# Block-causal attention and two MLPs on one core: attention scores of the later queries as three f32r products, under a new planned order

## The chip, the cores and the metric

The kernel runs on one core of one Trainium2 chip. The metric is the device time of one execution in microseconds, as the median of repeated runs. A profile of one execution gives the rows that are read below.

## The reference

Attention over 4 batches, 8 heads, 576 positions and head width 64, with a mask that is causal by blocks of 64 positions. Its output goes through an MLP with softplus and then through a second MLP with a softmax-weighted activation (SoLU) and a layer norm. All of it is in f32.

```python
scores = scale * np.matmul(q, k.transpose(0, 1, 3, 2))          # [4, 8, 576, 576], scale = 1/8
mask = block_i >= block_j                                        # blocks of 64
scores = np.where(mask, scores, -1000000000.0)
attn = np.exp(scores - np.max(scores, axis=-1, keepdims=True))
attn = attn / (np.sum(attn, axis=-1, keepdims=True) + 1e-09)
x = np.matmul(attn, v)                                           # then (2304 tokens, 512)
h = x @ w_in                                                     # 512 -> 2048
g = np.maximum(h, 0.0) + np.log1p(np.exp(-np.abs(h)))
y = g @ w_out                                                    # 2048 -> 512
h = y @ w_in2                                                    # 512 -> 1024
e = np.exp(h - max(h)); sm = e / (sum(e) + 1e-09); solu = h * sm
ln = (solu - mean(solu)) / np.sqrt(var(solu) + 1e-06) * g_ln
out = ln @ w_out2                                                # 1024 -> 512
```

## The kernel before

The work is cut into tasks, each a few instructions of one engine. A planner (`Plan.run`) takes every task with a duration, its dependencies and a rank, plays the engines forward in time, and always gives a free engine the ready task of lowest rank. The result is one fixed order for each engine's queue. A rank is a number of the task's group (`RANK`: a start and a step per unit), plus an offset of the function (`OFF`), plus a local number. So the tables `RANK` and `OFF` at the head of the file set the order of everything, and each queue then runs in order.

The MLP matmuls are f32r products of split numbers: a value is held as a high part rounded to f32r and a low part that is the rest, and a product is high x high, high x low and low x high, accumulated in PSUM. The weights are split on the chip in `Piece`: one load on SyncE's queue, an Abs on ScalarE, three bit operations on VectorE, a rounding copy and a subtraction.

The stages, in order of time:

- Units A (16, one for each batch and pair of heads): attention of the queries 0 to 255. At the same time the 32 pieces of the first MLP's weights are split, and the first pairs of the MLP run.
- Units C (16): attention of the queries 256 to 575. Each handles two heads that sit in partitions 0 to 63 and 64 to 127 of one tile, `qkC`, of 960 columns: 256 columns of q for the blocks 0 and 1 of 128 queries, 128 columns for the last 64 queries of both heads, laid out block-diagonally, and 576 columns of k. Block 0 (i = 0) sees 384 keys, block 1 sees 512, block 2 (i = 2, the block 8 of 64 queries of both heads) sees 576.
- Pairs (72): two rows of 128 of the first MLP's hidden width for a chunk of 256 tokens: `a` is w1 x (tile `hp`), then softplus on ScalarE and VectorE, then `b` (tile `acc`). They are in the queues between the steps of the attention from early on, since their ranks stand behind those of the units.
- Pieces U1 and U2 split the second MLP's weights, once the units C have freed their memory (`open_u`). Then come 18 steps `Tok` of 128 tokens each: `h`, the SoLU and norm, a transpose, and `op`.

Inside a unit C the path is: load `qkC` (two buffers), scores (`mm_qk`) into the one score tile `S` of two PSUM banks, mask, row maximum (`max`, line 406), exponent with its sum (`exp`, line 416), reciprocal, scaling (`norm`), transpose on TensorE through the one tile `T` (`tr`), copy to `ps`, product with v into `O` (`pv`), and the split of the result into the MLP's input `xt`. In blocks 0 and 1 the two heads write one bank each, from 64 rows each. All of it is plain f32 on TensorE. Line 203 is the helper `mm` that records nearly every matmul, line 209 and line 211 are the helper `copy` on ScalarE and VectorE.

Of the kernel before, what the change touches and what calls it, by code (L numbers as in the profile page):

```python
# [11 lines left out]
F32R = mybir.dt.float32r  # L12
I32 = mybir.dt.int32
AF = mybir.ActivationFunctionType
ALU = mybir.AluOpType
AX = mybir.AxisListType
# [2 lines left out]


OFF = {
    "Pair.a": -64.28, "Pair.b": 5.61, "Pair.do_gh": -507.04, "Piece.bits0": 97.37, "Piece.do_lo@P": -245.38,
    "Piece.do_lo_g": 483.40, "Tok.a": 249.83, "Tok.x_hi": -287.82, "UnitA.x_hi": 218.85, "Tok.tr": -74.68,
    "Tok.bm": 218.59, "UnitC.pv": 72.58, "UnitC.tr": -127.84, "Pair.stt": -176.06, "Pair.do_gl": -341.89,
}
RANK = {
# [3 lines left out]
    "Tok": (3472.49, -21.973),  # L30
}
MARGIN = {
    "PE": 600.0, "ACT": 100.0, "DVE": 100.0, "POOL": 100.0,
# [2 lines left out]
B, H, S, D = 4, 8, 576, 64  # L36
# [9 lines left out]
WC = (384, 512, 576)  # L46
# [5 lines left out]
class Plan:  # L52
# [8 lines left out]
    def add(self, eng, dur, rank, fn, deps=(), lat=None):  # L61
        t = _Task()
        t.key = key_of(fn)

        t.alts = dict(eng) if isinstance(eng, dict) else {eng: dur}
        name, i = t.group = self.group
        t.local = rank
        t.rank = rank + RANK[name][0] + RANK[name][1] * i + OFF.get(t.key, 0.0) + OFF.get(t.key + "@" + name, 0.0)
        t.eng, t.fn, t.n, t.done = None if len(t.alts) > 1 else eng, fn, len(self.tasks), False
        t.lat = (self.LAT + (120.0 if eng == "PE" else 0.0)) if lat is None else lat  # L70
        t.users, t.left, t.ready = [], 0, 0.0
        for d in deps:
            if d is not None:
                d.users.append(t)
                t.left += 1
        self.tasks.append(t)
        return t
# [5 lines left out]
    def chain(self, eng, rank, steps, deps):  # L83
        for dur, fn in steps:
            t = self.add(dur if isinstance(dur, dict) else eng, dur, rank, fn, deps)
            deps = [t]
        return t
# [83 lines left out]
def key_of(fn):  # L171
    while isinstance(fn, partial):
        fn = fn.func
    return ".".join(fn.__qualname__.split(".")[-2:])


def act_ns(n):
    return 70.0 + 0.833 * n


def dve_ns(n, per=1.04):
    return 70.0 + per * n
# [6 lines left out]
def dma_ns(nbytes, n=1):  # L189
    return max(50.0 + nbytes / 360.0, 550.0 * n)  # L190
# [3 lines left out]
def body(ctx: ExitStack, tc: tile.TileContext, qk, qkA, vP, vA, w1, w2, u1, u2, gln, out):  # L194
    nc = tc.nc
    PE, ACT, DVE, POOL, SP = nc.tensor, nc.scalar, nc.vector, nc.gpsimd, nc.sync
    plan = Plan()
    XTB, LAG = 3, 2
    add, chain = plan.add, plan.chain
    DMA_LAT = 1700.0  # L200

    def mm(out, lhsT, rhs, start, stop):
        PE.matmul(out, lhsT, rhs, start=start, stop=stop, skip_group_check=True)  # L203
# [3 lines left out]
    def copy(e, out, a):  # L207
        if e == "ACT":
            ACT.activation(out, a, AF.Copy)  # L209
        else:  # L210
            ENG[e].tensor_copy(out, a)  # L211

    def at_of(lst, i):
        return lst[i] if 0 <= i < len(lst) else None
# [15 lines left out]
    state = {}  # L230
# [88 lines left out]
    def xfree(c):  # L319

        return [t for u in pairs if u.c == c - XTB for t in (u.t_a0, u.t_a1)]
# [3 lines left out]
    class UnitC:  # L325
# [6 lines left out]
        def plan(self, prev, opened):  # L332
            p1, p2 = at_of(prev, len(prev) - 1), at_of(prev, len(prev) - 2)

            def g(u, *names):
                return [getattr(u, x) for x in names] if u else []

            self.t_qk = add("SP", dma_ns(128 * 3840), -12, self.load_qk, [opened] + g(p1, "t_qk") + g(p2, "t_mm"), DMA_LAT)
            self.t_v = add("SP", dma_ns(327680), -8, self.load_v, [opened, self.t_qk] + g(p2, "t_pv") + g(p1, "t_v"), DMA_LAT)
            sfree, tfree = (p1.sfree, p1.tfree) if p1 else ([], [])  # L340
            self.t_tr, cps = [[], [], []], []
            for i, w in enumerate(WC):
                r, heads = 7.0 * i, (0, 1) if i < 2 else (0,)
                self.t_mm = t = add("PE", (800, 1000, 1060)[i], r, partial(self.mm_qk, i), [self.t_qk] + sfree)
                if i < 2:
                    t = add("DVE", 140, r, partial(self.mask, i), [t])
                t = chain("DVE", r, ((dve_ns(w * len(heads)), partial(self.max, i)), (140, partial(self.scale, i))), [t])
                sfree = []
                for j in heads:
                    sfree.append(add("ACT", 250 + .833 * w, r, partial(self.exp, i, j), [t] + sfree + (p1.t_tr[i] if p1 else [])))  # L350
                t = chain("DVE", r, ((140, partial(self.den0, i)), (140, partial(self.den1, i))), sfree)
                for j in heads:
                    n = add("DVE", 70 + .55 * w, r, partial(self.norm, i, j), [t])
                    for part in ((0,) if i < 2 else (0, 1)):
                        m = 3 + i if i < 2 else (4, 1)[part]
                        x = add("PE", 60 + 110 * m, r + 5, partial(self.tr, i, j, part), [n] + tfree)
                        self.t_tr[i].append(x)
                        c = add({"ACT": 110 + 107 * m, "DVE": 90 + 133 * m}, None, r + 4, partial(self.copy, i, j, part), [x] + g(p1, "t_pv"))
                        tfree = [c]
                        cps.append(c)  # L360
            self.sfree, self.tfree = sfree, tfree
            self.t_pv = add("PE", 2272, 24, self.pv, cps + [self.t_v] + (p1.t_x if p1 else []))
            self.t_x, ta, tb, done = [], None, None, 0
            while done < NB:
                c, off = divmod(self.b * NB + done, CT)
                c += B
                w = min(NB - done, CT - off)
                args = (c, off, done, w)
                ta = add({"ACT": act_ns(w) + 40, "DVE": dve_ns(w)}, None, 22, partial(self.x_hi, *args), [self.t_pv, ta] + xfree(c))
                tb = add("DVE", dve_ns(w), 22, partial(self.x_lo, *args), [ta, tb])  # L370
                xparts.setdefault(c, []).append(tb)
                self.t_x.append(tb)
                done += w
            prev.append(self)

        def load_qk(self):

            self.qk = self.t([128, 960], "qkC")
            SP.dma_start(out=self.qk, in_=qk[self.b, self.pr])

        def load_v(self):
            self.v = self.t([128, 2, 5, D], "v")
            SP.dma_start(out=self.v, in_=vP[self.b, :, 2 * self.pr:2 * self.pr + 2])

        def scores(self, i):
            S, w = state["S"], WC[i]
            return S[:, :, 0:w] if i < 2 else S.rearrange("p a b -> p (a b)")[:, None, 0:w]

        def mm_qk(self, i):
            S, w, qk = state["S"], WC[i], self.qk  # L390
            if i < 2:
                for j in range(2):
                    h = slice(64 * j, 64 * j + 64)
                    mm(S[:, j, 0:w], qk[h, 128 * i:128 * i + 128], qk[h, 384:384 + w], True, True)
            else:
                mm(S[:, 0, :], qk[:, 256:384], qk[:, 384:896], True, True)
                mm(S[:, 1, 0:64], qk[:, 256:384], qk[:, 896:960], True, True)

        def mask(self, i):

# [2 lines left out]
        def max(self, i):  # L403
            self.m, self.den = self.t([128, 2], "mC", 3), self.t([128, 2], "dC", 3)
            n = 2 if i < 2 else 1
            DVE.tensor_reduce(out=self.m[:, 0:n], in_=self.scores(i), axis=AX.X, op=ALU.max, negate=True)  # L406
            self.n = n

        def scale(self, i):
# [3 lines left out]

        def exp(self, i, j):
            m, den, _ = self.stat[i]
            ACT.activation(state["eC"][i][:, j, :], self.scores(i)[:, j, :], AF.Exp, scale=0.125,  # L416
                           bias=m[:, j:j + 1], accum_out=den[:, j:j + 1])

        def den0(self, i):
            _, den, n = self.stat[i]  # L420
# [327 lines left out]
    for kind, f in todo:  # L748
        src, t, done = (w1[f], w1t[f], w1ready) if kind == "w1" else (w2[f * 128:f * 128 + 128, :], w2t[f], w2ready)
        p = Piece(src, w_of(t, 0), w_of(t, 1))  # L750
# [23 lines left out]
    for f in range(8):  # L774
        p = Piece(u1[f], u1_of(0, f), u1_of(1, f))
# [4 lines left out]
    for f in range(8):  # L780
        p = Piece(u2[f * 128:f * 128 + 128, :], w_of(w1t[6 + f], 0), w_of(w1t[6 + f], 1), gcol[:, f:f + 1])
        n = len(upieces) % 3
# [226 lines left out]
```

## Time and profile before

| | |
|---|---|
| Time, median of 3 runs | 818.53 us (815.85 to 818.89) |
| The profiled execution's own time | 818.25 us |
| Span of its instructions | 816.5 us |
| Time around the span | 1.75 us |
| Mean granted TensorE clock, as a share of 2.4 GHz | 0.991 |

The rows of the trace speak of the span. An f32 matmul stands in the rows as two matmul instructions and two weight loads (PEld), an f32r matmul as one of each; both types are labelled f32 there, so the tile names tell them apart: `S`, `T`, `O` and the tiles `R` and `r` of the units A hold f32 products, `hp`, `acc`, `h` and `op` f32r ones. A matmul's duration in a row is longer than the distance to the next one, since matmuls overlap; the distance of the starts is what a matmul costs.

### The profile page before, as it was taken

Reading aid. Unit: us, or ns where it says so; the run is one execution under the profiler, and the core shown is the slowest. Engines: PE = TensorE matmul, PEld = TensorE weight load, DVE = VectorE, ACT = ScalarE, POOL = GpSimd, SP = SyncE. Lnnn points to the kernel's source line nnn. Section 1 sums busy time; section 2 is a strip of 40 time slices with the busy share of each in tenths; the row PEclk is TensorE's granted clock in tenths of the full one; section 3 lists DMA queues with packets and bytes.
Section 4 is the critical chain, followed back from the end, with each engine's and each line's share of the span. In section 5 each row is a group of like instructions: output and inputs, shape, how many; then the busy total and the mean of one; then the engine's idle time right before and its main releaser. Section 6 shows DMA issues by size and latency. Waiting matters only on the chain.

```text
span 816.5 us, 14229 instructions
## 1 busy us (share of the span) xinstructions
PE 790.5 (97%) x5656; PEld 684.6 (84%) x5656; DVE 546.0 (67%) x1273; ACT 391.9 (48%) x863; POOL 0.7 (0%) x6
## 2 busy tenths in 40 slices
PE   5689999999999999999999999999999999999998
PEld 3478889998888788888887889999988888888887
DVE  6989999575666665665565652776949576766661
ACT  5566775554555545455554543645623232322232
POOL 0000000000000000000000000000000000000000
PEclk9799999999999999999999999999999999999999
DMA  5636551202121112112211100326301111110001
GB/s 166 214 119 192 175 165 63 92 10 79 49 83 41 42 42 67 41 42 71 61 41 41 58 3 26 105 78 207 117 27 39 51 39 53 39 51 27 26 26 51
DMA packets 31201, 59.63 MB, mean 73 GB/s; under 512 B 2848, under 2 KB 14368, under 8 KB 31136
## 3 DMA queue, kind: packets, MB, share of 16 engines
q1 hardware_dynamic: 31136, 58.74, 22.5%
q8 instruction: 44, 0.72, 0.4%
q14 instruction: 21, 0.17, 0.1%
HBM read 49.29 MB, written 9.44 MB: 72 GB/s over the span
## 4 chain that ended last, share of the span: by engine, by line
PE 80%; DVE 13%; DMA 3%; ACT 2%; issue 2%; SPq 0%; ACTq 0%; DVEq 0%
PE hp L203 19%; PE acc L203 18%; PE op L203 12%; PE h L203 11%; PE S L203 6%; PE O L203 5%; PE T L437 4%; PE tp L905 2%; PE R L203 2%; DVE a L283 2%; DMA raw<-in_w_dram 2%; DVE a L279 1%; DVE t L641 1%; DVE gl L649 1%; PE r L203 1%
## 5 line engine op out<-in xcount | busy, mean ns | idle before, releaser
L203 PE MATMUL hp<-xt,w 128*128 128x256 f32 x1728 | 218.9, 281 | 1.1 <-DVE t L641 1.0
L203 PEld LDWEIGHTS hp<-xt,w 128*128 128x128 f32 x1728 | 205.9, 189 | 5.4 <-issue 3.4
L203 PE MATMUL acc<-gh,w 128*128 128x256 f32 x768 | 150.3, 286 | 0.0
L203 PEld LDWEIGHTS acc<-gh,w 128*128 128x128 f32 x768 | 122.4, 189 | 13.0 <-issue 12.5
L203 PE MATMUL acc<-gl,w 128*128 128x256 f32 x384 | 107.0, 279 | 0.6 <-DVE gl L649 0.6
L203 PE MATMUL op<-w,w2w 128*128 128x512 f32 (+1 forms) x456 | 102.3, 381 | 0.0
L203 PE MATMUL h<-u,w 128*128 128x512 f32 x432 | 100.9, 390 | 0.0
L203 PEld LDWEIGHTS h<-u,w 128*128 128x128 f32 x432 | 80.7, 188 | 16.5
L203 PEld LDWEIGHTS op<-w,w2w 128*128 128x128 f32 x456 | 81.5, 188 | 15.3
L632 ACT ACTIVATE t<-hp 128x512 f32<-128x512 f32 x72 | 42.9, 596 | 79.3 <-PE hp L203 74.5
L209 ACT ACTIVATE ps<-T 128x512 f32<-128x512 f32 (+1 forms) x77 | 42.7, 554 | 75.0 <-PE T L437 60.3
L203 PEld LDWEIGHTS acc<-gl,w 128*128 128x128 f32 x384 | 72.7, 189 | 0.8 <-DVE gl L649 0.8
L641 DVE SCALAR_TENSOR_TENSOR t<-hp,t 128x512 f32<-128x512 f32 x72 | 49.4, 686 | 26.4 <-ACT t L638 26.0
L416 ACT ACTIVATE eC<-S,mC 128x384 f32<-128x384 f32 (+2 forms) x80 | 51.7, 653 | 11.6 <-DVE mC L410 11.5
L406 DVE TENSOR_REDUCE mC<-S 128x2 f32<-128x768 f32 (+2 forms) x48 | 46.9, 976 | 7.9 <-PE S L203 7.2
L203 PE MATMUL S<-qkC 64*128 64x384 f32 (+2 forms) x192 | 51.9, 533 | 0.0
L649 DVE TENSOR_TENSOR gl<-t,gh 128x512 fp32r<-128x512 f32 x72 | 49.6, 689 | 2.8 <-ACT gh L209 1.5
L203 PE MATMUL acc<-gh,w2w 128*128 128x256 f32 x256 | 50.2, 285 | 0.9 <-DVE gh L211 0.7
L857 ACT ACTIVATE e<-h,mx 128x1024 f32<-128x1024 f32 x18 | 20.1, 1116 | 55.1 <-PE tp L905 48.6
L203 PEld LDWEIGHTS acc<-gh,w2w 128*128 128x128 f32 x256 | 40.5, 188 | 6.9 <-issue 5.5
L638 ACT ACTIVATE t<-t 128x512 f32<-128x512 f32 x72 | 45.4, 630 | 2.0
L635 ACT ACTIVATE t<-t 128x512 f32<-128x512 f32 x72 | 45.4, 631 | 1.1
(149 smaller groups left out, 1050.4 us busy)
## 6 DMA issues: line engine op xcount, KB each, us to landing
raw<-in_w_dram SPq DMA_DIRECT2D x32, 512.0 KB, 3.9
qkC<-in_qk_dram SPq DMA_DIRECT2D x16, 480.0 KB, 3.4
raw_u<-in_u_dram SPq DMA_DIRECT2D x11, 512.0 KB, 3.5
v<-in_vP_dram SPq DMA_DIRECT2D x16, 320.0 KB, 3.0
x2s<-stg SPq DMA_DIRECT2D x18, 256.0 KB, 2.2
xr<-x2s SPq DMA_DIRECT2D x18, 256.0 KB, 3.1
qkA<-in_qkA_dram SPq DMA_DIRECT2D x16, 256.0 KB, 3.3
out_dram<-ob SPq DMA_DIRECT2D x15, 256.0 KB, 2.0
```

The source lines that it names most:

```text
L203: PE.matmul(out, lhsT, rhs, start=start, stop=stop, skip_group_check=True)
L209: ACT.activation(out, a, AF.Copy)
L283: DVE.scalar_tensor_tensor(out=self.a, in0=self.raw[:, :, 0], scalar=29, in1=self.a, op0=ALU.logical_shift_right, op1=ALU.bitwise_or)
L406: DVE.tensor_reduce(out=self.m[:, 0:n], in_=self.scores(i), axis=AX.X, op=ALU.max, negate=True)
L416: ACT.activation(state["eC"][i][:, j, :], self.scores(i)[:, j, :], AF.Exp, scale=0.125, bias=m[:, j:j + 1], accum_out=den[:, j:j + 1])
L437: PE.transpose(T[:, 128 * k:128 * k + 128], e[:, 128 * k:128 * k + 128], ident)
L632: ACT.activation(self.t, self.hp, AF.Abs)
L635: ACT.activation(self.t, self.t, AF.Exp, scale=-1.0)
L638: ACT.activation(self.t, self.t, AF.Ln, bias=1.0)
L641: DVE.scalar_tensor_tensor(out=self.t, in0=self.hp, scalar=0.0, in1=self.t, op0=ALU.max, op1=ALU.add)
L649: DVE.tensor_sub(self.gl, self.t, self.gh)
L857: ACT.activation(self.e, self.hh, AF.Exp, bias=self.mx, accum_out=self.ss)
```

## The change

In the units C, q and k are split after their load into a high part (`qk_hi`, a rounding copy of 960 columns on ScalarE or VectorE, as the planner finds) and a low part (`qk_lo`, a subtraction of 960 columns on VectorE). Raw tile, high part and low part have one buffer each, where the raw tile had two. The load of the next unit's tile waits for this unit's low part. The high part of the next unit waits for the last score matmul of this one.

Each score product becomes three f32r products, high x high, high x low, low x high, alternating between the two heads in blocks 0 and 1. Block 2's 576 keys are halved: 288 columns in each of the two banks, where 512 stood in one and 64 in the other. Maximum and exponent of block 2 read the two halves through one pattern. The planner's durations for the three score steps are new, and so are nearly all numbers of `RANK` and `OFF`.

The units A keep plain f32 scores. The diff:

```diff
@@ -19,15 +19,16 @@
 
 
 OFF = {
-    "Pair.a": -64.28, "Pair.b": 5.61, "Pair.do_gh": -507.04, "Piece.bits0": 97.37, "Piece.do_lo@P": -245.38,
-    "Piece.do_lo_g": 483.40, "Tok.a": 249.83, "Tok.x_hi": -287.82, "UnitA.x_hi": 218.85, "Tok.tr": -74.68,
-    "Tok.bm": 218.59, "UnitC.pv": 72.58, "UnitC.tr": -127.84, "Pair.stt": -176.06, "Pair.do_gl": -341.89,
+    "Pair.a": -160.87, "Pair.b": -32.19, "Pair.do_gh": -103.91, "Piece.bits0": 139.36, "Piece.do_lo@P": -201.40,
+    "Piece.do_lo_g": 267.76, "Tok.a": 141.06, "Tok.x_hi": -460.68, "UnitA.x_hi": 408.37, "Tok.tr": -394.45,
+    "Tok.bm": 359.77, "UnitC.pv": 348.22, "UnitC.tr": -288.31, "Pair.stt": -191.35, "Pair.do_gl": -445.21,
+    "UnitC.qk_lo": -290.12,
 }
 RANK = {
-    "first": (278.93, 20.397), "A0": (-641.43, 96.996), "A1": (-4066.20, 24.379), "A2": (-152.64, -0.844),
-    "A3": (-1221.38, -173.545), "P0": (3437.70, -107.962), "P": (247.97, -35.750), "C": (692.49, 11.636),
-    "Pair0": (7.78, -1.510), "Pair": (1879.52, 20.653), "U1": (2411.63, 26.547), "U2": (1151.70, -31.129),
-    "Tok": (3472.49, -21.973),
+    "first": (278.93, 20.397), "A0": (636.85, 83.080), "A1": (-4008.02, 57.487), "A2": (-200.66, 24.018),
+    "A3": (-1158.93, -177.493), "P0": (3522.23, -182.270), "P": (108.24, -25.537), "C": (1333.72, -23.955),
+    "Pair0": (-27.93, 4.604), "Pair": (1577.17, 27.249), "U1": (3142.36, 101.962), "U2": (864.20, 12.958),
+    "Tok": (4285.47, -27.327),
 }
 MARGIN = {
     "PE": 600.0, "ACT": 100.0, "DVE": 100.0, "POOL": 100.0,
@@ -335,13 +336,15 @@
             def g(u, *names):
                 return [getattr(u, x) for x in names] if u else []
 
-            self.t_qk = add("SP", dma_ns(128 * 3840), -12, self.load_qk, [opened] + g(p1, "t_qk") + g(p2, "t_mm"), DMA_LAT)
+            self.t_qk = add("SP", dma_ns(128 * 3840), -12, self.load_qk, [opened] + g(p1, "t_ql"), DMA_LAT)
+            self.t_qh = add({"ACT": act_ns(960), "DVE": dve_ns(960, .52)}, None, -6, self.qk_hi, [self.t_qk] + g(p1, "t_mm"))
+            self.t_ql = add("DVE", dve_ns(960), -6, self.qk_lo, [self.t_qh])
             self.t_v = add("SP", dma_ns(327680), -8, self.load_v, [opened, self.t_qk] + g(p2, "t_pv") + g(p1, "t_v"), DMA_LAT)
             sfree, tfree = (p1.sfree, p1.tfree) if p1 else ([], [])
             self.t_tr, cps = [[], [], []], []
             for i, w in enumerate(WC):
                 r, heads = 7.0 * i, (0, 1) if i < 2 else (0,)
-                self.t_mm = t = add("PE", (800, 1000, 1060)[i], r, partial(self.mm_qk, i), [self.t_qk] + sfree)
+                self.t_mm = t = add("PE", (600, 760, 860)[i], r, partial(self.mm_qk, i), [self.t_ql] + sfree)
                 if i < 2:
                     t = add("DVE", 140, r, partial(self.mask, i), [t])
                 t = chain("DVE", r, ((dve_ns(w * len(heads)), partial(self.max, i)), (140, partial(self.scale, i))), [t])
@@ -375,26 +378,34 @@
 
         def load_qk(self):
 
-            self.qk = self.t([128, 960], "qkC")
-            SP.dma_start(out=self.qk, in_=qk[self.b, self.pr])
+            self.qr = self.t([128, 960], "qkC", 1)
+            SP.dma_start(out=self.qr, in_=qk[self.b, self.pr])
+
+        def qk_hi(self, e):
+            self.qk = [state["pat"].tile([128, 960], F32R, tag=x, name=x, bufs=1) for x in ("qkh", "qkl")]
+            copy(e, self.qk[0], self.qr)
+
+        def qk_lo(self):
+            DVE.tensor_sub(self.qk[1], self.qr, self.qk[0])
 
         def load_v(self):
             self.v = self.t([128, 2, 5, D], "v")
             SP.dma_start(out=self.v, in_=vP[self.b, :, 2 * self.pr:2 * self.pr + 2])
 
         def scores(self, i):
+
+            return state["S"][:, :, 0:WC[i] if i < 2 else WC[2] // 2]
+
+        def mm_qk(self, i):
             S, w = state["S"], WC[i]
-            return S[:, :, 0:w] if i < 2 else S.rearrange("p a b -> p (a b)")[:, None, 0:w]
-
-        def mm_qk(self, i):
-            S, w, qk = state["S"], WC[i], self.qk
-            if i < 2:
+            for n, (a, b) in enumerate(((0, 0), (0, 1), (1, 0))):
+                q, k = self.qk[a], self.qk[b]
                 for j in range(2):
-                    h = slice(64 * j, 64 * j + 64)
-                    mm(S[:, j, 0:w], qk[h, 128 * i:128 * i + 128], qk[h, 384:384 + w], True, True)
-            else:
-                mm(S[:, 0, :], qk[:, 256:384], qk[:, 384:896], True, True)
-                mm(S[:, 1, 0:64], qk[:, 256:384], qk[:, 896:960], True, True)
+                    if i < 2:
+                        h = slice(64 * j, 64 * j + 64)
+                        mm(S[:, j, 0:w], q[h, 128 * i:128 * i + 128], k[h, 384:384 + w], n == 0, n == 2)
+                    else:
+                        mm(S[:, j, 0:w // 2], q[:, 256:384], k[:, 384 + w // 2 * j:384 + w // 2 * (j + 1)], n == 0, n == 2)
 
         def mask(self, i):
 
@@ -403,7 +414,7 @@
         def max(self, i):
             self.m, self.den = self.t([128, 2], "mC", 3), self.t([128, 2], "dC", 3)
             n = 2 if i < 2 else 1
-            DVE.tensor_reduce(out=self.m[:, 0:n], in_=self.scores(i), axis=AX.X, op=ALU.max, negate=True)
+            DVE.tensor_reduce(out=self.m[:, 0:n], in_=self.scores(i), axis=AX.X if i < 2 else AX.XY, op=ALU.max, negate=True)
             self.n = n
 
         def scale(self, i):
@@ -413,8 +424,12 @@
 
         def exp(self, i, j):
             m, den, _ = self.stat[i]
-            ACT.activation(state["eC"][i][:, j, :], self.scores(i)[:, j, :], AF.Exp, scale=0.125,
-                           bias=m[:, j:j + 1], accum_out=den[:, j:j + 1])
+            e, sc = state["eC"][i][:, j, :], self.scores(i)
+            if i < 2:
+                sc = sc[:, j, :]
+            else:
+                e = e.rearrange("p (a b) -> p a b", a=2)
+            ACT.activation(e, sc, AF.Exp, scale=0.125, bias=m[:, j:j + 1], accum_out=den[:, j:j + 1])
 
         def den0(self, i):
             _, den, n = self.stat[i]
```

## Rows read from the trace of the kernel before

**Rows 1.** The page, part 1: busy us (share of the span) and instructions.
```profile
PE 790.5 (97%) x5656; PEld 684.6 (84%) x5656; DVE 546.0 (67%) x1273; ACT 391.9 (48%) x863; POOL 0.7 (0%) x6
```

**Rows 2.** The page, part 4: the chain that ended last, by engine and by line.
```profile
PE 80%; DVE 13%; DMA 3%; ACT 2%; issue 2%; SPq 0%; ACTq 0%; DVEq 0%
PE hp L203 19%; PE acc L203 18%; PE op L203 12%; PE h L203 11%; PE S L203 6%; PE O L203 5%; PE T L437 4%; PE tp L905 2%; PE R L203 2%; DVE a L283 2%; DMA raw<-in_w_dram 2%; DVE a L279 1%; DVE t L641 1%; DVE gl L649 1%; PE r L203 1%
```

**Rows 3.** Windows by stage: length, engines' busy us, PE clock, DMA share, GB/s.
```profile
0.00:130.00 130.00, 108.56 (x833) 93.68 (x834) 118.00 (x292) 84.16 (x201) 0.70 (x6) 0.95 0.53 172
...
191.60:505.50 313.90, 313.90 (x2450) 262.07 (x2449) 184.88 (x470) 162.02 (x364) 0.00 (x0) 1.00 0.15 44
505.50:606.10 100.60, 99.40 (x843) 97.86 (x842) 73.58 (x133) 53.33 (x90) 0.00 (x0) 1.00 0.33 108
```

**Rows 4.** The chain in one unit C's period: start us, us, what.
```profile
316.11 0.84 PE S L203 x4
...
322.06 1.06 PE S L203 x4
...
328.30 1.03 PE S L203 x4
329.33 1.47 PE hp L203 x12
...
335.00 0.85 PE S L203 x4
```

**Rows 5.** Timeline of TensorE at score blocks 0 and 1: start us, us, what.
```profile
316.04 0.59 PE L203 MATMUL S<-qkC 64*128 64x384 f32 x2
316.47 0.49 PE L203 MATMUL S<-qkC 64*128 64x384 f32 x2
316.89 0.38 PE L203 MATMUL acc<-gh,w 128*128 128x256 f32 x1
...
321.99 0.70 PE L203 MATMUL S<-qkC 64*128 64x512 f32 x2
322.52 0.60 PE L203 MATMUL S<-qkC 64*128 64x512 f32 x2
323.05 0.38 PE L203 MATMUL acc<-gh,w 128*128 128x256 f32 x1
```

**Rows 6.** Timeline of the weight loads at score block 0.
```profile
316.04 0.30 PEld L203 LDWEIGHTS S<-qkC 64*128 64x128 f32 x4
```

**Rows 7.** The chain in two dense stretches of f32r matmuls, 256 and 512 columns.
```profile
541.10 2.72 PE hp L203 x24
...
712.25 5.45 PE h L203 x24
```

**Rows 8.** Lines by form: VectorE and ScalarE passes like the new ones.
```profile
L649 DVE TENSOR_TENSOR gl<-t,gh 128x512 fp32r<-128x512 f32 x72 | 49.6, 689 | 2.8 <-ACT gh L209 1.5
L211 DVE CAST gh<-t 128x512 fp32r<-128x512 f32 x56 | 23.7, 424 | 22.4 <-PE acc L203 21.3
L860 DVE TENSOR_TENSOR e<-h,e 128x1024 f32<-128x1024 f32 x18 | 22.0, 1222 | 6.6 <-ACT e L857 6.6
L857 ACT ACTIVATE e<-h,mx 128x1024 f32<-128x1024 f32 x18 | 20.1, 1116 | 55.1 <-PE tp L905 48.6 <-DVE mx L852 6.3
L209 ACT ACTIVATE gh<-t 128x512 fp32r<-128x512 f32 x16 | 10.1, 630 | 5.3 <-PE acc L203 4.4 <-DVE t L641 0.8
```

**Rows 9.** Timeline of VectorE behind score block 2 (idle before, released by).
```profile
329.37 0.76 DVE L406 TENSOR_REDUCE mC<-S 128x1 f32<-128x576 f32 x1 [0.48 <-PE S L203]
```

**Rows 10.** Loads of the units C: time from issue to landing.
```profile
DMA to landing us min/median/max: 3.1/3.4/4.4
```

**Rows 11.** Tile views raw_u, u, op: ns min/median/max, first and last start us.
```profile
L268 SPq DMA_DIRECT2D raw_u<-in_u_dram x11: 327/328/618, 505.6 to 580.9; - x11
...
L293 DVE TENSOR_TENSOR u<-a_u,u x8: 681/692/693, 513.8 to 557.2; 128x512 fp32r<-128x512 f32 x8
...
L203 PE MATMUL op<-w,w2w x456: 277/389/476, 641.4 to 813.0; 128*128 128x512 f32 x136, 128*128 128x256 f32 x16
```

## The prediction

> **What bounds the kernel now.** I read the busy shares first: TensorE is busy for 790.5 of 816.5 us, VectorE for 67%, ScalarE for 48% [rows 1]. The chain that ended last says the same: 80% of it is TensorE, and 13% VectorE [rows 2]. But a share over the span mixes stages, so the windows come next [rows 3]. In the first 130 us TensorE is idle for 21.4 us (130 less 108.56) while VectorE works for 118.0 of 130: that stage waits for the splitting of the weights. From 191.6 to 505.5 us, where all 16 units C lie, TensorE's records leave no gap, at full granted clock, while VectorE has 184.9 us of work in 313.9 (59%) and ScalarE 162.0 (52%). So there a microsecond of TensorE work is a microsecond of time, and one of VectorE's or ScalarE's is not, as long as it comes in time. What follows, pairs until 606 us and the second MLP, is TensorE's too, and it moves forward as a block when the units C end earlier. The score matmuls are in the chain with 6% [rows 2]: 0.84, 1.06 and 1.03 us for the three blocks of a unit [rows 4], 2.93 us, times 16 is 46.9 us. This is what the change can reach.
>
> **TensorE, blocks 0 and 1.** An f32 product is two passes. In block 0 both heads' first passes are recorded from 316.04, the second from 316.47, and the next work's load from 316.89; in block 1 the marks are 321.99, 322.52 and 323.05 [rows 5]. From first to second pass it takes 0.43 us for 384 columns and 0.53 for 512: 0.10 us for 128 columns, some 0.83 ns a column, so 0.32 and 0.43 us a pass, and 0.11 us over, the first weight load. After the second pass 0.10 us remain, in which the array changes from 64-row tiles to 128. Block 0 is then 0.11 + 2 x 0.32 + 0.10 = 0.85, block 1 is 0.11 + 2 x 0.43 + 0.10 = 1.07 (1.06 in the rows). The two heads share this time: their passes start together, and the four loads are done in 0.30 us [rows 6].
>
> An f32r matmul costs 2.72 / 24 = 0.113 us for 256 columns and 5.45 / 24 = 0.227 for 512 [rows 7], 0.443 ns a column, own load hidden. That is 0.170 us for 384 and 0.227 for 512. If the two heads still run side by side, block 0 becomes 0.11 + 3 x 0.170 + 0.10 = 0.72 (0.13 less), and block 1 0.11 + 3 x 0.227 + 0.10 = 0.89 (0.17 less).
>
> **TensorE, block 2.** It uses all 128 rows. Six f32r matmuls of 288 columns cost 6 x 288 x 0.443 ns = 0.765 us, against 1.03 now: 0.265 less. The piece behind it, 12 matmuls of a pair, takes 1.47 us [rows 4] where 12 x 0.113 = 1.36 is normal: the old block ends with 64-column passes too short to hide the next load. Six equal matmuls should hide it, so up to 0.11 more, 0.375 in all. I take the middle, 0.32.
>
> The sum is 0.13 + 0.17 + 0.32 = 0.62 us a unit, 9.9 us for 16 units; with the bounds of block 2, 9.0 to 10.8.
>
> **A rule against this.** In these rows the second pair of loads of block 0 is done 0.30 us after the first began [rows 6], while the first passes, in the same rows of the array, run until 316.47 [rows 5]; and 24 f32r matmuls with a load each keep 0.113 us [rows 7]. A load thus hides behind a running matmul of its own rows. The Trainium skill, "TensorE: Matmul & The Clock Gate", section "Part 3: Packing small matmuls — row/col tiling", says that weight loads overlap matmuls in flight only when the row group differs. By that each of the 18 new products would show its load of 0.11: block 0 0.94, block 1 1.11, block 2 1.42, together 0.45 us a unit more than now (1.12 taken for block 2 with the load behind it), and the kernel would take about 825. The rows contradict it, so it gets no chance of its own.
>
> **VectorE and ScalarE.** Added per unit is one subtraction of 960 columns. Between 689 ns for 512 and 1222 for 1024 [rows 8] it comes to 689 + 448/512 x 533 = 1155 ns. The rounding copy is, on VectorE, between 424 ns (512 columns) and 795 (that times 960/512); I take 0.7. On ScalarE it is 630 + 448/512 x (1116 - 630) = 1.06 us [rows 8]. That is 18.5 us of subtractions and at most 12.7 of copies on VectorE, 216 us in about 304, 71%; no engine becomes the bound. Maximum and exponent of block 2 read the same 576 elements; I cost the other pattern at nothing, since their order has cover.
>
> The cover of the split is the time from a unit's last score matmul to the next unit's first: 329.3 to 335.0, 5.7 us [rows 4], full of pair and attention work. The copy waits for that last matmul, the subtraction for the copy, the score matmul for the subtraction. A handover costs between 0.04 us (block 2 ends at 328.30 + 1.03 = 329.33 [rows 4], its maximum starts at 329.37) and the 0.48 us that VectorE sat idle in front of that maximum [rows 9]. So 0.7 to 1.06, plus 1.16, plus three times that is 2.0 to 3.7 us, and at least 2.0 us are spare. Behind copy and subtraction VectorE's queue holds block 2's maximum, so that exponent can come up to 1.9 us later, and after it the next unit's first scores, for the same tile `S`. If the cover were gone altogether, each unit would stall by up to 1.9 us, 30 us in all. TensorE has pairs for the space, in the planned order, so I count zero.
>
> The load now has one buffer and waits for the previous unit's subtraction. It is issued about a unit ahead (some 18 us) and lands in 3.4, at most 4.4 us [rows 10]; SyncE's other transfers have the same time. Zero.
>
> **The new order.** Units C still rank before pairs, pairs fill. If the units stretch, fewer pairs remain to cover the second MLP's weights. Their loads start at 505.6, the first matrix is split by 558, and its transfers go on past 580.9, yet pairs last until 606 and `op` first runs at 641.4 [rows 11]; some 30 us of delay would pass unseen. In the first 130 us the order decides how much of the 21.4 us of idle TensorE remains [rows 3]. The rows of before don't show the new order, and both tables order the same VectorE work of 118 us there. I take zero, with bounds: 6 us either way, something over a quarter of the idle time.
>
> **The sum.** 818.25 (the profiled execution; 816.5 span and 1.75 around it) less 9.9 is 808.35. The median of the runs is 0.28 above that execution, so 808.6.
>
> **Rivals.**
>
> *The heads don't run side by side in f32r* (other side). In f32 each head delivers a column in 0.83 ns, two together one in 0.42; in f32r side by side it would be one in 0.22, a rate that no row shows. If the array's output stays at one column in 0.443 ns, block 0 costs 0.21 + 6 x 0.170 = 1.23 (0.38 more), block 1 0.21 + 6 x 0.227 = 1.57 (0.51 more), block 2 still 0.32 less: 0.57 a unit, 9.1 us, 827.7. It turns to a loss once blocks 0 and 1 together cost 0.32 more than now. For it speaks that missing row, against it that the heads have separate rows, loads and banks. The Trainium skill, "PSUM — Partial Sum Buffer", section "🔬 PSUM: the matmul accumulator", says that TensorE's only way out is one PSUM write port, which would make this case; no run here shows either yet. Chance 0.10.
>
> *The split arrives late, or the new order gives time back.* If VectorE's queue makes the split outlast its spare time by 0.2 to 0.5 us in each unit, or the first stage loses as much in one piece, 3 to 8 us of the gain go: 812 to 816.5; at 0.62 us a unit all of it. For it: VectorE rises to 71%, and in the first stage it is nearly always busy. Against: 2.0 us spare, and pairs as filler. Chance 0.14.
>
> *The new order also shortens the first stage*, by 5 us or more of the 21.4: 798 to 804. Chance 0.08.
>
> *My forecast*, 804 to 812: chance 0.68.
>
> **The numbers.** About 0.5% (4.1 us) is what a measurement tells from no change: faster is below 814.4, slower above 822.6. Forecast, the shorter first stage and two thirds of the second rival are faster, 0.85; I lower it to 0.80 for costs that I don't see. Same 0.09, slower 0.11. The range is 802 to 816: it leaves out the first rival's 0.10 and some 0.06 at the ends.
>
> **What would show it.** Right: blocks of about 0.72, 0.89 and 0.77 us in the chain, both heads' f32r products starting in pairs, no idle of TensorE in the units C, 32 new passes of about 1.16 us and 0.7 to 1.06 us. Wrong: starts of the two heads one product apart; TensorE idle in front of `S` and released by the subtraction; a first stage of 130 us that grows; the units C ending as late as before with TensorE's gaps in them.

## The result

The changed kernel takes 810.92 us (median of 4 runs, 808.6 to 811.84), the kernel before 817.40 in the same count. The ratio is 0.9915, with a 95% interval of 0.9894 to 0.9935: 0.85% faster. The forecast was 808.6 in a range of 802 to 816, faster with 0.80. The direction and the mechanism came out; of the 9.9 us, about 6.5 arrived. Seen in the profiled executions, it is 818.25 to 811.79.

The page of the changed kernel, part 1 (as [rows 1]):

```profile
PE 783.8 (97%) x5752; PEld 694.7 (86%) x5752; DVE 568.3 (70%) x1291; ACT 394.0 (49%) x877; POOL 0.7 (0%) x6
```

TensorE's busy time falls by 6.7 us although it has 96 more matmuls, VectorE's rises by 22.3 us without becoming the bound. The stages cut at the first score matmul, the last product with v and the first `op`, first of the kernel before, then of the changed one (length, busy us of TensorE, weight loads, VectorE, ScalarE, GpSimd; clock; DMA share; GB/s):

```profile
0.00:191.63 191.63, 170.12 (x1360) 150.94 (x1361) 157.37 (x387) 115.64 (x280) 0.70 (x6) 0.96 0.42 136
191.63:505.31 313.68, 313.68 (x2449) 261.95 (x2448) 184.88 (x470) 162.02 (x364) 0.00 (x0) 1.00 0.15 44
505.31:641.35 136.04, 134.84 (x1012) 127.38 (x1013) 100.82 (x192) 64.60 (x115) 0.00 (x0) 1.00 0.29 94
641.35:816.47 175.12, 171.90 (x841) 144.29 (x839) 102.96 (x225) 49.67 (x104) 0.00 (x0) 1.00 0.12 40
```

```profile
0.00:192.88 192.88, 171.58 (x1384) 152.88 (x1385) 157.62 (x383) 119.96 (x289) 0.70 (x6) 0.96 0.42 135
192.88:498.66 305.78, 305.78 (x2544) 271.13 (x2544) 206.76 (x490) 161.22 (x372) 0.00 (x0) 1.00 0.16 47
498.66:634.89 136.23, 134.54 (x989) 126.38 (x989) 100.94 (x194) 63.15 (x113) 0.00 (x0) 1.00 0.28 90
634.89:810.02 175.13, 171.90 (x841) 144.34 (x839) 103.01 (x225) 49.67 (x104) 0.00 (x0) 1.00 0.12 40
```

The units C got 7.90 us shorter, still without a gap on TensorE. The end is the same to 0.01 us. In the other two stages work moved: 24 pair matmuls went from behind the units C to before them (1360 to 1384 matmuls, 1012 to 989), 24 x 0.113 = 2.7 us. So in these two profiles the first stage, 1.25 us longer, really gained 1.5, and the stage behind the units, 0.19 us longer, really lost 2.9: -1.5 - 7.9 + 2.9 = -6.5.

One period of the units C in the chain of the changed kernel (as [rows 4]: start us, us, what):

```profile
311.61 2.35 PE O L204 x20
313.96 1.61 PE hp L204 x12
315.57 0.80 PE S L204 x6
316.37 0.33 PE T L452 x3
...
319.96 1.38 PE acc L204 x12
321.34 0.72 PE S L204 x6
322.06 0.58 PE T L452 x4
...
327.20 0.89 PE S L204 x6
328.10 0.23 PE T L449
...
334.00 0.80 PE S L204 x6
```

The score blocks cost 0.72, 0.89 and 0.80 us, 2.41 a unit where it was 2.93: 0.52 less, 8.3 us over 16 units. The period from block 2 to block 2 is 18.43 us, where block 0 to block 0 was 18.89 [rows 4].

TensorE's timeline at block 0 and the new tiles' instructions:

```profile
321.26 0.44 PE L204 MATMUL S<-qkh 64*128 64x384 f32 x2
321.55 0.34 PE L204 MATMUL S<-qkl,qkh 64*128 64x384 f32 x2
321.72 0.34 PE L204 MATMUL S<-qkh,qkl 64*128 64x384 f32 x2
```

```profile
L389 DVE TENSOR_TENSOR qkl<-qkC,qkh x16: 1147/1148/1159, 187.9 to 465.1; 128x960 fp32r<-128x960 f32 x16
L212 DVE CAST qkh<-qkC x15: 649/660/661, 187.3 to 463.8; 128x960 fp32r<-128x960 f32 x15
L210 ACT ACTIVATE qkh<-qkC x1: 1008/1008/1008, 224.3 to 224.3; 128x960 fp32r<-128x960 f32 x1
```

Each product of the two heads stands as one pair (x2), 0.17 us behind the pair before it (321.72 less 321.55). The subtraction takes 1.148 us, the copy 0.66 on VectorE and 1.01 on ScalarE.

### The profile page after: what moved, and what is told of

Read it like the earlier page. It is cut to its first block, busy times and chain, and to the rows that moved or that the text cites. A ratio compares the mean times of both kernels' runs of the same rounds, so it can differ in the third digit from the quotient of the medians.

```text
span 810.0 us, 14410 instructions
## 1 busy us (share of the span) xinstructions
PE 783.8 (97%) x5752; PEld 694.7 (86%) x5752; DVE 568.3 (70%) x1291; ACT 394.0 (49%) x877; POOL 0.7 (0%) x6
## 4 chain that ended last, share of the span: by engine, by line
PE 81%; DVE 8%; DMA 6%; ACT 3%; issue 1%; SPq 0%; ACTq 0%; DVEq 0%
PE hp L204 20%; PE acc L204 18%; PE op L204 12%; PE h L204 11%; PE S L204 5%; PE O L204 5%; PE T L452 4%; DMA raw_u<-in_u_dram 2%; DMA raw<-in_w_dram 2%; PE R L204 2%; PE tp L920 2%; PE r L204 1%; DVE a L284 1%; DVE eA L564 1%; DVE a L280 1%
## 5 line engine op out<-in xcount | busy, mean ns | idle before, releaser
L204 PE MATMUL hp<-xt,w 128*128 128x256 f32 x1728 | 221.6, 284 | 3.7 <-DVE t L656 3.4
L204 PE MATMUL acc<-gh,w 128*128 128x256 f32 x768 | 148.1, 284 | 0.0
L210 ACT ACTIVATE ps<-T 128x512 f32<-128x512 f32 (+1 forms) x74 | 40.8, 551 | 51.7 <-PE T L452 50.1
L452 PE MATMUL T<-ident,eC 128*128 128x128 f32 x288 | 45.3, 275 | 0.0
L926 ACT ACTIVATE w2w<-tp 128x512 fp32r<-128x512 f32 x36 | 20.7, 596 | 46.2 <-PE op L204 41.4
```

Of the source, the lines that this page charges most:

```text
L452: PE.transpose(T[:, 128 * k:128 * k + 128], e[:, 128 * k:128 * k + 128], ident)
L926: ACT.activation(self.lh[:, 4 * g:4 * g + 4, :], self.tp[g], AF.Copy)
```

## The experiments

Ratios are to the kernel before, in runs on the same chip. "Units C" is the stretch from the first score matmul to the last product with v, "behind" the one from there to the first `op`.

**The order and the split apart: e1_old_tables and e2_new_tables.** Theory 1 is that of the prediction: the time follows TensorE's work in the scores. Theory 2: the new order brings the gain. The first kernel is the whole change with the old numbers, the second the old kernel with the new numbers:

```diff
 OFF = {
-    (the numbers of the changed kernel)
+    (the numbers of the kernel before)
 RANK = {
-    (the numbers of the changed kernel)
+    (the numbers of the kernel before)
```

> The whole change, but with the rank and offset tables of before. Theory 1 (the time follows TensorE's work in the scores, the tables give about nothing): the three score blocks at 0.72, 0.89 and 0.80 us as in the changed kernel, 16 x 0.5 = 8 us less than before, 808 to 812. Theory 2 (the new order brings the gain, the split by itself pays for itself): 815 to 819, with TensorE waiting in the units C or behind them.

> The kernel before (f32 scores), with the new rank and offset tables. Theory 1: blocks at 0.84, 1.06 and 1.03 us, time within 2 us of before, 815 to 820. Theory 2: about 811.

Measured: with the old tables 811.44 us, 0.9931 (0.9913 to 0.9948); the old scores with the new tables 818.12 us, 1.0019 (1.0005 to 1.0033). Their units C, first the one, then the other:

```profile
192.51:499.57 307.06, 307.06 (x2556) 272.37 (x2556) 201.00 (x492) 172.94 (x368) 0.00 (x0) 1.00 0.16 48
```

```profile
189.96:504.81 314.85, 314.85 (x2460) 263.22 (x2460) 183.91 (x463) 168.09 (x373) 0.00 (x0) 1.00 0.15 44
```

Theory 2 falls. The split brings the gain, with either table; the new order by itself is not faster than the old one, 0.2% slower if anything. (Each of these stretches holds 12 pair matmuls more than that of its scores in the other table, 1.4 us.)

**A product less: e3_two_products.**

```diff
-            for n, (a, b) in enumerate(((0, 0), (0, 1), (1, 0))):
+            for n, (a, b) in enumerate(((0, 0), (0, 1))):
```

(and the last product is then n == 1).

> The changed kernel without the product of q's low part with k's high part, so the scores lack that term. Theory 1: 0.17 + 0.23 + 2 x 0.133 = 0.66 us less per unit, 10.6 us, about 800.5. A rival (the units C are held by their chain over VectorE and ScalarE, or the covering work behind them runs short): less than half of it, 806 to 811, with TensorE idle in front of the scores or behind the units C.

Measured: 802.61 us, 0.9825 (0.9802 to 0.9849), 8.3 us less than the changed kernel's 810.92. The units C and the stage behind them:

```profile
193.36:488.61 295.25, 295.25 (x2448) 261.31 (x2448) 206.47 (x490) 161.22 (x372) 0.00 (x0) 1.00 0.17 49
488.61:627.60 138.99, 135.98 (x988) 128.47 (x989) 100.75 (x194) 63.11 (x113) 0.00 (x0) 0.99 0.27 88
```

The units C got 10.5 us shorter (305.78 to 295.25), as the sum of the products said (10.6). Up to there nothing but TensorE's work counts. But the stage behind grew from 136.23 to 138.99 with the same matmuls: in this execution part of what is won in the units is given back behind them. The waits of TensorE in that stage (us, times, longest) show on what, first here, then in the changed kernel:

```profile
PE hp L204 <- DVE t L656: 3.0, 2, 2.4
```

```profile
PE hp L204 <- DVE t L656: 1.4, 2, 1.0
```

And the clock takes its part. Behind the longest of these waits (2.35 us of idle TensorE) the granted clock is 0.50, 1.2 GHz, for 3.4 us, and 24 matmuls take 4.62 us where 2.72 [rows 7] to 2.83 is usual. The timeline there, and the window:

```profile
547.06 4.62 PE L204 MATMUL hp<-xt,w 128*128 128x256 f32 x24 [2.35 <-DVE t L656]
```

```profile
547.50:550.90 3.40, 3.40 (x18) 3.40 (x17) 2.06 (x5) 2.02 (x4) 0.00 (x0) 0.50 0.93 370
```

So the stage lost 1.6 us more by waiting and about 1.8 us by the clock, 3.4 us against the 2.8 by which it grew; the two profiles differ in more than that. This profiled execution was the slowest of its four runs (804.52 us).

**The heads in turn: e4_heads_in_turn.** Blocks 0 and 1 with the loops over products and heads exchanged:

```diff
-            for n, (a, b) in enumerate(((0, 0), (0, 1), (1, 0))):
-                q, k = self.qk[a], self.qk[b]
-                for j in range(2):
+            order = [(n, j) for j in range(2) for n in range(3)] if i < 2 else [(n, j) for n in range(3) for j in range(2)]
+            for n, j in order:
+                q, k = self.qk[T[n][0]], self.qk[T[n][1]]
```

> The changed kernel with the three products of one head issued before the three of the other in blocks 0 and 1. If the two heads run side by side (theory 1), the queue lets only the last product of the first head overlap the first of the second: five product times instead of three, 0.34 us more in block 0 and 0.45 in block 1, 12.7 us in all, about 824. If they were one after the other all along (the rival of the prediction): no change, about 811.

Measured: 810.97 us, 0.9932 (0.9914 to 0.9950): no change. Taken alone that would be the rival's answer, but the timeline says otherwise. The order in which the kernel issues the six matmuls of block 0, then TensorE's timeline of one such block:

```
L204 MATMUL S<-qkh 128x384
L204 MATMUL S<-qkl,qkh 128x384
L204 MATMUL S<-qkh,qkl 128x384
L204 MATMUL S<-qkh 128x384
L204 MATMUL S<-qkl,qkh 128x384
L204 MATMUL S<-qkh,qkl 128x384
```

```profile
304.41 0.45 PE L204 MATMUL S<-qkh 64*128 64x384 f32 x2
304.69 0.34 PE L204 MATMUL S<-qkl,qkh 64*128 64x384 f32 x2
304.87 0.34 PE L204 MATMUL S<-qkh,qkl 64*128 64x384 f32 x2
```

The second head's first product is the fourth in the program, but it starts with the first one (each x2 is one matmul of either head), and so on by pairs. The block takes 0.73 us. So the heads do run side by side in f32r, and my expectation was wrong about the queue, not about the array.

**The split twice: e5_low_twice.**

```diff
             DVE.tensor_sub(self.qk[1], self.qr, self.qk[0])
+            DVE.tensor_sub(self.qk[1], self.qr, self.qk[0])
```

> The changed kernel with the subtraction for the low parts done twice in each unit C (1.15 us more of VectorE, 18.4 us in all, in the path from the load to the scores). If the split is covered in the units C: their stretch stays at 306 us and the time at 811, within 2 us. The rival (VectorE's queue holds the units C up): up to 18 us more, TensorE idle in front of S.

Measured: 811.58 us, 0.9918 (0.9894 to 0.9942). The units C:

```profile
194.38:500.30 305.92, 305.92 (x2544) 271.13 (x2544) 223.63 (x505) 160.23 (x372) 0.00 (x0) 1.00 0.16 48
```

VectorE has 16.9 us more to do than in the changed kernel (206.76), and the stretch is 0.14 us longer. The split is covered, and at least another 1.15 us in its path would be.

**Less of VectorE behind the units: e6_u_bits_out.**

```diff
         def bits1(self):
+            if self.get is conv_u:
+                return
```

> The changed kernel without one of the three bit operations (the sign) in the splitting of the second MLP's weights, so these weights lose their sign: 16 x 0.6 = 9.6 us less of VectorE behind the units C. If what was given back there (2.9 us) is pairs that wait for VectorE, the stretch from the last product with v to the first op gets 2 to 3 us shorter, 808 to 809. The rival (the loads of these weights, or the order by itself, make the wait): less than 1 us.

Measured: 809.82 us, 0.9904 (0.9874 to 0.9933), an interval that holds the changed kernel's ratio. Behind the units, this kernel and then the changed one profiled again (e9, below):

```profile
497.09:631.45 134.36, 134.34 (x989) 127.25 (x989) 91.55 (x178) 63.07 (x113) 0.00 (x0) 1.00 0.28 91
```

```profile
499.30:634.04 134.74, 134.36 (x989) 126.98 (x989) 100.66 (x194) 63.16 (x113) 0.00 (x0) 1.00 0.27 91
```

VectorE's 9.1 us less shorten the stage by 0.38 us, which is all the idle time that TensorE's records leave there (134.74 less 134.36). So the amount of VectorE's work is not what costs most behind the units; the expectation of 2 to 3 us was wrong. What costs more there is told below, where the prediction is gone through.

**Block 2 uncut: e7_block2_uncut.**

```diff
-                        mm(S[:, j, 0:w // 2], q[:, 256:384], k[:, 384 + w // 2 * j:384 + w // 2 * (j + 1)], n == 0, n == 2)
+                        mm(S[:, j, 0:(512, 64)[j]], q[:, 256:384], k[:, 384 + 512 * j:(896, 960)[j]], n == 0, n == 2)
```

(and maximum and exponent read one row of 576 again).

> The changed kernel with block 2 in 512 and 64 columns, as before the change, and in f32r. 64 columns of f32r are too short to hide a load of 0.11 us: 3 x (0.227 + 0.11) = 1.01 us for the block instead of 0.80, 3.4 us in all, about 814. If loads always hide, 3 x 0.255 = 0.77 and no change.

Measured: 813.48 us, 0.9950 (0.9932 to 0.9967). Its block 2 in the chain, and the transposes behind it:

```profile
314.69 0.94 PE S L204 x6
315.64 0.36 PE T L450 x3
```

0.94 us instead of 0.80, between the two values expected (1.01 and 0.77), and 0.03 more behind it; the units C are 308.75 us long instead of 305.78, 3.0 us. The halving of the keys is worth more than a third of the 7.9 us gained in the units.

**Another order: e8_new_order, with e9_after_again and e10_new_order_again.** The planned queues were played forward with the durations of the traces, and the numbers of `RANK`, `OFF` and `MARGIN` were changed at random and kept when the play ended earlier (a few numbers of the result):

```diff
-    "Tok.bm": 359.77, "UnitC.pv": 348.22, "UnitC.tr": -288.31, "Pair.stt": -191.35, "Pair.do_gl": -445.21,
+    "Tok.bm": 21257.52, "UnitC.pv": -6000.77, "UnitC.tr": -6165.03, "Pair.stt": -15884.59, "Pair.do_gl": -20398.90,
...
-    "PE": 600.0, "ACT": 100.0, "DVE": 100.0, "POOL": 100.0,
+    "PE": 362.1, "ACT": 137.6, "DVE": 112.7, "POOL": 6839.4,
```

> The changed kernel with rank, offset and margin tables found by playing the planned queues with the durations of the traces (0.72, 0.89, 0.80 us for the scores, 1.36 us for half a pair, VectorE and ScalarE as planned) and looking for the earliest end. That play ends 3.7 us earlier than with the changed kernel's tables, 2.4 of them in the first stage, 1.3 behind the units C: 806 to 809. If the play leaves out what matters, 811 or more.

> The changed kernel itself, beside the next one on the same chip: 810 to 812. Its profile says how much of the 2.9 us behind the units C was this one execution: about 1.6, as in the kernels with the same order, if the rest was one late load.

> The kernel with the tables found by the play, again: 808 to 810, 1.5 to 3 us less than the changed kernel in the same call, if the earlier difference was its order and not the chip.

Measured: 808.89 us, 0.9896 (0.9872 to 0.9921) the first time. The second time it took 808.12 us, 0.9878 (0.9860 to 0.9896), beside the changed kernel's 811.50, 0.9930 (0.9914 to 0.9945): 3.4 us faster than the changed kernel, with intervals that don't touch. The first two stages of the second profile:

```profile
0.00:190.03 190.03, 168.50 (x1373) 149.86 (x1374) 154.07 (x381) 120.38 (x291) 0.70 (x6) 0.96 0.40 133
190.03:496.45 306.42, 306.42 (x2544) 270.89 (x2544) 208.18 (x501) 156.14 (x361) 0.00 (x0) 1.00 0.17 50
```

Against e9 the first stage is 3.5 us shorter (193.52 to 190.03) with 12 pair matmuls less (1.4 us), the units C 0.6 us longer. But the changed kernel's own order had first stages of 192.88 to 194.40 us in four of the profiles (the changed kernel, e3, e4, e9), and of 191.31 and 190.84 in e6 and e7; the edits of e3, e4, e6 and e7 act no earlier than the first score matmul. And the two profiled executions are only 1.9 us apart as wholes (809.18 and 807.30 us). One profile can't say how much of the 3.4 us is won there.

## Why the prediction was right, and where its size was off

**Bound by TensorE in the units C: right.** The stretch has no gap before and after, a product less shortened it by what the product costs (e3), and a second subtraction changed nothing (e5).

**Blocks 0 and 1: right.** Forecast 0.72 and 0.89 us, measured 0.72 and 0.89. The rival with heads one after the other falls: both heads deliver a column in some 0.45 ns at the same time (384 columns each, pairs 0.17 us apart). The Trainium skill, "PSUM — Partial Sum Buffer", section "🔬 PSUM: the matmul accumulator", has one PSUM write port as TensorE's only way out; read as one column at a time it is contradicted here, by these pairs.

**Block 2: the term that was mis-sized.** I took 0.32 us a unit, as the middle of 0.265 and 0.375. The block went from 1.03 to 0.80, 0.23. Six matmuls of 288 columns cost 0.133 us each, not the 0.1275 that the dense stretches gave. The load behind the block is hidden, as the upper bound had it: the transposes behind it take 0.33 us as elsewhere. But the period didn't keep that: 18.89 less 18.43 is 0.46 us, less than the blocks' 0.52. In the changed kernel pairs follow the product with v (tile `O`), and these 12 matmuls take 1.61 us where 1.38 is normal, 0.23 more at the change of the array's tiles. In the period shown before, block 0 followed that product, and its first load, 0.11 us, was counted in the block:

```profile
332.65 2.35 PE O L203 x20
335.00 0.85 PE S L203 x4
```

With the split and the old tables (e1) pairs follow it as well, and the piece takes 1.61 us there too, so this comes with the split and not with the new numbers. And the pairs in the units C run at a slower pace for longer than before, which costs 0.6 us (the two paces are shown below). So in the units C 7.9 us came instead of 9.9.

**The split: right.** 1.148 us for the subtraction (1.155 forecast), 0.66 and 1.01 for the copy (0.7 and 1.06), VectorE at 206.76 of 305.78 us, 68% (71%).

**Nothing lost behind the units: wrong.** The prediction had all that follows the units C move forward as a block, and took the new order at zero. In the profiled execution 2.9 us went there. About half of that was lost where pairs wait for softplus in VectorE's queue. VectorE at that place, then TensorE:

```profile
568.16 0.43 DVE L277 TENSOR_SCALAR a_u<-a_u 128x512 int32<-128x512 int32 x1 [0.79 <-ACT a_u L274]
...
571.73 0.42 DVE L277 TENSOR_SCALAR ob<-ob 128x512 int32<-128x512 int32 x1
572.07 0.68 DVE L656 SCALAR_TENSOR_TENSOR t<-hp,t 128x512 f32<-128x512 f32 x1
```

```profile
572.81 0.97 PE L204 MATMUL hp<-xt,w 128*128 128x256 f32 x6 [0.96 <-DVE t L656]
```

VectorE first waits 0.79 us for a piece of the second MLP's weights, and the softplus step of line 656 stands behind the pieces' operations in its fixed order; the next pair's matmuls wait 0.96 us for it. Profiled again (e9), the same program took 134.74 us for this stage, 1.5 us less: the late piece was that execution's. What stays is 134.74 against 136.04 with 2.7 us less of pairs, 1.4 us lost.

This 1.4 us is not waiting: TensorE's waits in this stage add up to 1.0 us in the kernel before and to 0.4 in e9. It is the pace of the pair matmuls themselves. The chain in this stage, first of the kernel before, then of e9, then of e6:

```profile
532.94 2.72 PE acc L203 x24
535.66 2.72 PE hp L203 x24
```

```profile
565.05 2.83 PE hp L204 x24
590.15 14.13 PE acc L204 x120
```

```profile
500.24 5.44 PE hp L204 x48
581.91 5.65 PE hp L204 x48
```

The same matmul of 256 columns costs 0.113 us in some stretches and 0.118 in others, at full granted clock in both (1.00 in the windows of this stage). Added up by the start distances in the traces, what the pairs of this stage take beyond 0.1133 us each is 0.5 us in the kernel before, 1.9 in the changed kernel's profile, 2.7 in e9 and 3.2 in e6. So in e9 the pace costs 2.2 us more than before, and fewer waits and gaps give 0.8 back. It fits e6 too: its waits are gone, but its pairs ran at the slower pace for longer. What sets the pace is not shown; it changes at a gap of 0.3 us in one place (e9, at 507.6) and at none in another (e9, at 548.2).

Nor is this loss shown to be the new order's. With the old tables and the split (e1) the stage takes 133.91 us with 36 pair matmuls less than before (4.1 us), so 2.0 us are lost there too.

**The balance** of two executions (e9 against the kernel before, 809.18 to 816.47): first stage 193.52 to 191.63 with 2.7 us more in it, -0.8, which is within the scatter of that stage (190.84 to 194.40 us with the changed kernel's order); units C -7.9; behind +1.4. Together -7.3 by the spans, and -6.5 by the medians.

## What to carry to other kernels

Where a stage is filled by one engine, sum its instructions by start distances from the trace: the blocks came out within 0.01 us where the form was the same, and were 0.035 us off in the one whose width was new. Here a static order that fills the time of one engine hid another 1.8 us of VectorE work a unit, and 1.15 us more of it in e5. What is won in the filled stage can be lost again behind it, by waits, by the clock behind a wait (e3), or by matmuls that run at a slower pace without any wait, so look there at what stands in front of whom in each queue, and at the cost of one matmul by stretches. When durations change, measure the new order by itself, against the same kernel with the old one: the change's own new tables brought nothing that the runs show (e1, e2), those of e8 brought 3.4 us.

## What the runs showed of the hardware that was not expected

Matmuls of different 64-row tiles are not held in program order: with three products of one head issued before the three of the other, the other's first one starts with the first (304.41, two matmuls as one pair), and the block takes 0.73 us as with alternating heads (e4). The Trainium skill, "TensorE: Matmul & The Clock Gate", section "Part 3: Packing small matmuls — row/col tiling", says that matmuls start and end strictly in program order; this trace differs, and the measurement decides.

A short f32r matmul costs more than its columns: three pairs of 512 and 64 columns took 0.94 us (e7), where 3 x 576 columns at 0.443 ns are 0.77.

A dense stretch of f32r matmuls has two paces at the same granted clock: 24 of 256 columns take 2.72 us or 2.83 (the chains above).

The first stage differed by up to 3.6 us between profiles of the same order (190.84 in e7, 194.40 in e4), before the edit of either is reached. Part of it goes with the granted clock: 1.2 GHz was granted for 6.8 us of this stage in e7, for 13.7 in e6, and for 17.1 in the changed kernel, e4 and e9. A difference of 1 to 3 us there can't be read from one profile.
